# Making the owners of the sorted columns behind the index, instead of ahead of it, in a fused RWKV-5 and switch-routing kernel

## The chip, the cores and the metric

The kernel runs on one core of a Trainium2 chip. The metric is the device time of one execution in microseconds (us), the lower the better. The kernel before was timed three times: 420.32 us in the median, 418.83 the lowest and 420.70 the highest. Its profiled execution took 419.83 us, of which 418.1 us lie between the first and the last instruction; all times "at" some point below count from that first instruction.

The engines are called PE (TensorE, matrix products; PEld is its weight load), DVE (VectorE), ACT (ScalarE), POOL (GpSimd) and SP (SyncE, which issues most of the DMA transfers).

## The reference, cut to what matters

Two blocks stand behind one another. The first is a linear recurrence over 768 steps for 4 batches, 8 heads and a head size of 48. Its output, seen as 3072 tokens of 384 numbers, goes through a gate that sends each token to one of 8 experts, and each expert is a two-layer network of its own weights.

```python
def _attn_ref(r, k, v, w, u):
    ...
    for t in range(S):
        cur = np.einsum('bhd,bhe->bhde', u[None] * kt, vt)
        y[:, :, t] = np.einsum('bhd,bhde->bhe', rt, state + cur)
        state = w[None, :, :, None] * state + np.einsum('bhd,bhe->bhde', kt, vt)
    return y

def _moe_ref(x, w_gate, w1, w2):        # x: 3072 x 384, w1: 8 x 384 x 1024, w2: 8 x 1024 x 384
    logits = x @ w_gate
    expert_idx = np.argmax(logits, axis=1)
    ...                                 # probs: a softmax of the logits
    gate_w = probs[np.arange(N), expert_idx]
    for e in range(E):
        mask = expert_idx == e
        xe = x[mask]
        h = np.maximum(xe @ w1[e], 0.0)
        ye = h @ w2[e]
        out[mask] = gate_w[mask, None] * ye
    return out
```

## The kernel before

The kernel runs the recurrence first, in 32 units, and writes its rows to a table in HBM, `x_hbm`. Then it sorts the tokens by expert and works on them in tiles of 128 tokens. The first two tiles, `t0` and `t1`, are chosen early, from the first half of the batches, and belong to experts 0 and 1, so their rows and weights are loaded while the recurrence still runs. All later tiles, from `t2` on, need the full sort. Two things come out of it on DVE:

- the **index** `idx`: for each column (a tile is one column) the token numbers of its 128 rows. It is built by 24 small matrix products and four DVE operations. The gathers of a tile's rows (POOL's indirect DMA) need it.
- the **owners** `ei`: for each column the expert that it belongs to. They are built by eight DVE operations on one partition. The load of a tile's first-layer weights `w1` (1536 KB) needs them, since SP reads the expert's number from `ei` to make the address; the second product reads the expert's number too, on PE, to pick its slice of `w2_all`.

```python
    def owners(self, rt, first):
        ef = rt.tile([1, NCOL], FP32, name="ef")
        tge = rt.tile([1, NTILE, E], FP32, name="tgo")
        nc.vector.tensor_tensor(tge, ..., op=ALU.is_ge)
        nc.vector.tensor_reduce(ef[:, 0:NTILE], tge, axis=AX, op=ALU.add)
        oe = rt.tile([1, E, E], FP32, name="oe")
        nc.vector.tensor_tensor(oe, self.own[0:1], ..., op=ALU.mult)
        nc.vector.tensor_reduce(ef[:, NTILE:], oe, axis=AX, op=ALU.add)
        self.ei = rt.tile([1, NCOL], I32, name="ei")
        nc.vector.tensor_scalar_min(self.ei, ef, float(E - 1))
        ...                                  # nf, twice, and nt: how many late tiles there are

    def to_index(self, pool, Bv, n, n_chunks, tag, nm):     # R.index calls this
        ...
        for g in range(n_chunks):
            nc.tensor.matmul(idp..., lhsT=self.At[:, g, :], rhs=Bv[:, g]..., ...)
        nc.vector.tensor_copy(idl, idp)                     # idxl
        nc.vector.tensor_scalar(out=emp, ...)               # idxe
        nc.vector.scalar_tensor_tensor(out=raw, ...)        # idxr
        nc.vector.scalar_tensor_tensor(out=idx, ...)        # idx

    def load_w1(self, wp, part=0):
        ...
            e = self.expert(ENG.SP)                         # reads ei on SP
            nc.sync.dma_start(self.w1, w1[ds(e, 1)]...)

    def turn(self, mo, tag, copy=nc.vector.tensor_copy):    # needs the rows xs
        for d in range(DT):
            nc.tensor.transpose(p[:, d, :], self.xs[:, 128 * d:128 * d + 128], ident)
        copy(self.xT, p)

    def hidden(self, mo, fb, within=None, at=2):            # needs xT and w1; fb is 0 or 1
        for f in range(4):
            if within and f == at:
                within()
            for d in range(DT):
                nc.tensor.matmul(p[:, f, :], lhsT=self.w1[:, q, d, o:o + 128], rhs=self.xT[:, d, :], ...)
        nc.scalar.activation(self.hT[:, 4 * fb:4 * fb + 4, :], p, func=ACT.Relu)

    def product(self, within=None):                         # needs hT and w2_all
        for f in range(FT):
            if within and f == FT - 2:
                within()
            nc.tensor.matmul(p, lhsT=self.hT[:, f, :], rhs=w2_all[:, e, f * DM:(f + 1) * DM], ...)

    def weigh(self, mo):                                    # yo, on DVE
        nc.vector.tensor_scalar_mul(self.y, self.p, self.xs[:, DM:W])
```

The seam between the recurrence and the tiles stands in the program in this order. The order of the statements is the order of the instructions on each engine.

```python
            t0.hidden(mo, 1)
            t1.turn(la, "g", nc.scalar.copy)
            R.bases(rt)
            R.order(rt)
            R.slots(rt)
            for step in R.onehots(B - 1):
                step()
            R.owners(rt, NSURE - NEARLY)
            t2.load_w1(wp)
            w2_load(E - 1)
            t0.product()
            t1.hidden(mo, 0, lambda: R.index(rt, "rw"), 3)
            t2.load_x(mo)
            t3.load_x(mo)
            t0.weigh(mo)
            t0.store()
            t1.hidden(mo, 1)
            R.segment_index()
            t3.load_w1(wp)
            t1.product(lambda: t2.turn(mo, "g"))
            t1.weigh(mo)
            t1.store()
            ...
            run_tiles(tiles[2:], ...)      # t2.hidden(0), t2.hidden(1), t3.turn, t2.product, ...
```

Of the kernel before, what the change touches and what calls it, by code (L numbers as in the profile page):

```python
# [20 lines left out]
E, F = 8, 1024  # L21
# [16 lines left out]
NSURE = NG  # L38
FQ = 4
FW = F // FQ  # L40
NEARLY = 2
# [12 lines left out]
def rwkv5_then_switch(ctx, tc, r, k, v, rk, tok, wu_in, wg, wgh, w1, w2, out):  # L54
# [38 lines left out]
    def load_rk(u):  # L93
        b, hf, hp = unit(u)
        if u < 4:
            nc.sync.dma_start(rks[u % 4], rk[b, hf, hp])
        else:
            for hi in range(2):
                q = slice(64 * hi, 64 * hi + D)
                nc.sync.dma_start(rks[u % 4][q], rk[b, hf, hp, q])  # L100

    def load_v(u):
        b, hf, hp = unit(u)
        nc.sync.dma_start(vs[u % 6][:, 0:2 * HC * D], tok[b, hf, hp, :, 0:2 * HC * D])

    def load_kt(u):
        b, hf, hp = unit(u)
        nc.sync.dma_start(kts[u % 4], tok[b, hf, hp, :, 2 * HC * D:])
# [118 lines left out]
    def w2_load(e, eng=nc.sync, q=slice(0, FQ)):  # L227
        eng.dma_start(w2_all[:, e, :].rearrange("p (q f) -> p q f", q=FQ)[:, q], w2[e, q].rearrange("q p f -> p q f"))
# [200 lines left out]
    def fast():  # L429
# [6 lines left out]
        wp = att.enter_context(tc.tile_pool(name="wp", bufs=1))  # L436
# [4 lines left out]
        R = Routes(ps, la, NEARLY)  # L441
# [25 lines left out]
        def scaled(out, tab, hp, by):  # L467
            nc.scalar.activation(out[:, hp, :], tab[:, hp, :], func=ACT.Copy, scale=by[:, hp:hp + 1])

        def tables(hp):  # L470
            scaled(W2, Wr, hp, w_64)
            scaled(W1, Wp, hp, w_64)

        def table_g():
            w3p = ps.tile([128, HP, C], FP32, name="w3p", tag="rw", bufs=1)
            for hp in range(HP):
                nc.tensor.transpose(w3p[:, hp, :], W3[:, hp, :], ident)
            nc.vector.tensor_copy(Wg, w3p.rearrange("p a (h d) -> p a h d", h=2)[:, :, :, 0:D])  # L478
# [23 lines left out]
        def u_scale_first(u):  # L502

            x = units[u]
            hp = x["hp"]
            if u:
                nc.vector.tensor_tensor(x["RK"], x["r"], x["k"], op=ALU.mult)
            for o, i, tab in (("K", "k", Wr), ("R", "r", Wp)):
                nc.vector.scalar_tensor_tensor(out=x[o], in0=x[i], scalar=w_64[:, hp:hp + 1],
                                               in1=bc(tab[:, hp, None, :], [128, HC, C]), op0=ALU.mult, op1=ALU.mult)  # L510
# [10 lines left out]
        def u_scale_g(u):  # L521
            x = units[u]
            hp, ns = x["hp"], x["ns"]
            nc.gpsimd.tensor_tensor(  # L524
                x["Kg"][:, 0:ns, :], x["kt"][:, 0:ns, :],
                bc(Wg[:, hp].rearrange("p h d -> p (h d)")[:, None, :], [128, ns, 2 * D]), op=ALU.mult)
# [32 lines left out]
        def u_scores(u, parts=(u_own, u_products, u_diagonal)):  # L559
            units[u]["P"] = [ps.tile([128, 512], FP32, name=f"P{hi}", tag=f"P{hi}", bufs=2) for hi in range(2)]  # L560
            for part in parts:
                part(u)

        def u_mask(u):
            x = units[u]
            A, P = x["A"], x["P"]
            for hi in range(2):
                nc.vector.copy_predicated(  # L568
                    A[:, hi], bc(mask[:, None, :].bitcast(I32), [128, HC, C]),
                    P[hi][:, 0:HC * C].rearrange("p (c t) -> p c t", t=C))  # L570
# [44 lines left out]
        def gate_weights():  # L615
            nc.gpsimd.memset(IW, 0.0)
            for hi in range(2):
                nc.sync.dma_start(IW[64 * hi:64 * hi + D, :, 2 * D:], wgh[hi])
# [56 lines left out]
        with tc.manual_schedule():  # L675
            u_scale_first(0)
            gate_weights()
            load_rk(4)
            load_v(4)
            for load in pieces[:AHEAD]:  # L680
                load()
            for hp in range(HP):
                scaled(W3, Wr, hp, pw[:, LV - 1])
            u_scores(0, (u_own, u_diagonal, u_products))
            tables(2)
            u_scale_first(1)
            R.begin()
            nc.vector.memset(Gp, 0.0)
            table_g()
            u_mask(0)  # L690
            u_scores(1, (u_own, u_diagonal, u_products))
            u_scale_g(0)
            load_kt(4)
            u_scale_g(1)
            for hp in (3, 0, 1):
                tables(hp)
            u_state(0)
            u_scale_r(2)
            idle(2)
            for u in range(NU):  # L700
                if u + 5 < NU:
                    load_rk(u + 5)
                    load_kt(u + 5)
                    load_v(u + 5)
                for load in piece.get(u, ()):
                    load()
                if u + 2 < NU:
                    u_scale_k(u + 2)
                    if u:
                        u_scale_r(u + 2)  # L710
                    u_scale_g(u + 2)
                if u == 0:
                    u_out(0)
                    u_mask(1)
                    u_state(1)
                elif u + 1 < NU:
                    u_scores(u + 1)
                    u_state(u + 1)
                    u_mask(u + 1)
                if u:  # L720
                    u_out(u)
                if u == 2:
                    gate_columns()
                if u >= HP and u % HP < HC:
                    u_gate(u // HP - 1, u % HP, "rw")
                for step in todo[u]:
                    step()
                for j in range(NEARLY):
                    if u == 2 * HP + j:
                        tiles[j].clear(la)  # L730
                    if u == NU - HP + 2 * j:
                        tiles[j].load_x(la)
            fr.close()
            t0, t1, t2, t3 = tiles[0:4]
            t0.turn(la, "g")
            for c, tag in enumerate(("rw", "y", "y")):
                u_gate(NU // HP - 1, c, tag)
            fy.close()
            rt = att.enter_context(tc.tile_pool(name="rt", bufs=1))
            mo = em.enter_context(tc.tile_pool(name="mo", bufs=2))  # L740
            shift, first, weight, rows = chosen[B - 1]
            product, *ranks = R.ranks(B - 1, "rw")
            shift()
            first()
            t0.hidden(mo, 0, product, 3)
            weight()
            rows(0, 2)
            rows(1, 2)
            for e in range(NW, E - 1):
                w2_load(e)  # L750
            for step in ranks:
# [5 lines that stand above are left out]
            R.slots(rt)  # L757
            for step in R.onehots(B - 1):
                step()
            R.owners(rt, NSURE - NEARLY)  # L760
            t2.load_w1(wp)
            w2_load(E - 1)
            t0.product()
            t1.hidden(mo, 0, lambda: R.index(rt, "rw"), 3)
            t2.load_x(mo)
            t3.load_x(mo)
            t0.weigh(mo)
            t0.store()
            t1.hidden(mo, 1)
            R.segment_index()  # L770
# [4 lines that stand above are left out]
            late = late_tiles_of(R, NSURE - NEARLY)  # L775
            run_tiles(tiles[2:], wp, mo, Segments(R, 0), zip(late, [xbs[1][:, i] for i in range(G)] + [t0.xs, t1.xs],
                                                             strict=True))
# [311 lines left out]
    class Segments(Tile):  # L1089
# [9 lines left out]
        def load(self, mo, i):  # L1099

            q = i % FQ
            if i == 0:
                self.es = [self.expert(ENG.SP, NTILE + self.j * NS + k) for k in range(NS)]
                self.w = {}
            self.w[i] = self.tile(mo, [128, NS, DT * FW], "wq", 2)
            for k, e in enumerate(self.es):
                src = w1[ds(e, 1), q].rearrange("a p d f -> p (a d f)") if i < FQ else \
                    w2[ds(e, 1), q].rearrange("a p f -> p (a f)")
                nc.sync.dma_start(self.w[i][:, k], src)
# [139 lines left out]
    with tc.If(usual > 0) as which:  # L1249
        fast()  # L1250
# [60 lines left out]
```

## Time and profile before

| | |
|---|---|
| median of three runs | 420.32 us |
| span of the profiled execution | 418.1 us |
| PE busy | 403.0 us, 96% of the span |
| PE on the chain of work that ended last | 89% of the span |
| DVE, ACT, POOL busy | 154.0, 127.4 and 151.2 us |
| bytes moved by DMA | 99.00 MB, mean 237 GB/s |
| granted clock of PE | 0.99 |

A profile line of the timeline reads: start, duration, engine, source line, operation, tile written <- tiles read, shapes, count, and in brackets the idle time of the engine before it and what ended that. Of the source lines, L961 to L974 are the owners, L859 the matrix products of the index and L862 to L870 its DVE operations, L1019 the load of `w1`, L228 a load of `w2`, L1040 the gather of a tile's rows, L1046 `turn`, L1061 `hidden`, L1072 `product` and L1076 `weigh`. The weights' tiles appear as `w1s` and `w_all`, the gathered rows as `xs`. The recurrence ends at about 127 us, and the seam lies between there and about 155 us.

### The profile page before, as it was taken

To read this page: it belongs to the slowest core of one execution; us is meant where nothing else is said; L and a number is where in the kernel's file an instruction comes from. 1 tells how busy PE (TensorE), PEld (TensorE's weight loads), DVE (VectorE), ACT (ScalarE), POOL (GpSimd) and SP (SyncE) were. 2 spreads that over 40 slices of the span, in tenths; PEclk is the share of its full clock that TensorE was granted. 3 is DMA by queue.
4 is the path that set the end of the run, shared out by engine and by line. 5 is a ranking of instruction groups with operands and counts; after the bars stand their busy time and mean duration, and the time that the engine had idled before them with its cause. 6 is when DMAs were issued, how large, how long until landed. Compare 5 with 4: busy or idle time off the path is not lost.

```text
span 418.1 us, 10368 instructions
## 1 busy us (share of the span) xinstructions
PE 403.0 (96%) x4057; PEld 333.6 (80%) x4057; DVE 154.0 (37%) x410; ACT 127.4 (30%) x395; POOL 151.2 (36%) x194
## 2 busy tenths in 40 slices
PE   7999999999999989999999999999999999999990
PEld 7899999999999767777788887777878786777770
DVE  6887899999977811111111111110111101111100
ACT  3787777776873211111111101011111100100110
POOL 6897679679750031121111222121222111110100
PEclk9999999999999999999999999999999999999996
DMA  7899999999992998568866686968767675455000
GB/s 247 251 253 261 276 273 302 289 279 297 303 259 102 337 385 311 189 231 328 317 191 221 209 310 201 337 197 294 231 240 249 237 263 188 171 185 173 31 24 27
DMA packets 42944, 99.00 MB, mean 237 GB/s; under 512 B 5189, under 2 KB 16474, under 8 KB 42882
## 3 DMA queue, kind: packets, MB, share of 16 engines
q1 hardware_dynamic: 39024, 86.94, 63.9%
q0 software_dynamic: 3712, 11.23, 9.3%
q8 instruction: 37, 0.61, 0.6%
q14 instruction: 25, 0.20, 0.2%
q10 hardware_dynamic: 146, 0.01, 0.0%
HBM read 88.72 MB, written 9.65 MB: 235 GB/s over the span
## 4 chain that ended last, share of the span: by engine, by line
PE 89%; DVE 4%; DMA 2%; POOL 1%; ACT 1%; issue 1%; POOLq 0%; DVEq 0%
PE hp L1061 29%; PE yp L1072 27%; PE P L536 6%; PE P L546 6%; PE yp L607 5%; PE yp L603 4%; PE rp L638 4%; PE Gp L582 3%; PE xTp L1046 2%; DMA xs<-x_hbm,idx 2%; PE hg L1124 1%; PE yg L1144 1%; DMA wu<-in_w_u_dram 0%; ACT A L557 0%; POOL w_all L443 0%
## 5 line engine op out<-in xcount | busy, mean ns | idle before, releaser
L1061 PEld LDWEIGHTS hp<-xT,w1s 128*128 128x128 f32 x1152 | 133.1, 192 | 10.4 <-issue 4.1
L1061 PE MATMUL hp<-xT,w1s 128*128 128x128 f32 x1152 | 135.2, 276 | 0.0
L1072 PE MATMUL yp<-w_all,hT 128*128 (+1 forms) x384 | 128.0, 486 | 0.0
L1072 PEld LDWEIGHTS yp<-w_all,hT 128*128 128x128 f32 x384 | 71.0, 190 | 44.2
L1063 ACT ACTIVATE hT<-hp 128x512 f32<-128x512 f32 x48 | 28.7, 597 | 230.8 <-PE hp L1061 230.8
L1083 POOL DMA_INDIRECT out_dram<-yo,idx x22 | 22.3, 1011 | 192.0 <-DVE yo L1076 182.5
L557 ACT ACTIVATE A<-ident,dv 128x128 f32<-128x128 f32 x192 | 59.6, 389 | 0.2 <-ACT dv L554 0.2
L1076 DVE TENSOR_SCALAR yo<-yp,xs 128x384 f32<-128x384 f32 x22 | 13.6, 618 | 106.5 <-PE yp L1072 106.5
L1048 DVE COPY xT<-xTp 128x384 f32<-128x384 f32 x23 | 12.8, 555 | 99.7 <-PE xTp L1046 99.7
L607 PE MATMUL yp<-A,w_all 128*64 128x128 f32 x384 | 38.4, 274 | 0.0
L518 POOL TENSOR_TENSOR w_all<-w_all 128x384 f32<-128x384 f32 x30 | 30.7, 1023 | 20.2 <-DMA w_all<-in_r_k_units_dram 4.8
L568 DVE COPY_PREDICATED A<-mask,P 128x384 f32<-128x384 int32 x64 | 35.7, 585 | 4.4 <-ACT A L557 4.0
L1040 POOL DMA_INDIRECT xs<-x_hbm,idx x22 | 21.3, 966 | 31.2 <-DVE yo L1076 24.8
L603 PE MATMUL yp<-w_all,St 128*64 128x128 f32 x320 | 31.9, 274 | 0.0
L519 POOL TENSOR_TENSOR w_all<-w_all,W 128x384 f32<-128x384 f32 x30 | 30.7, 1023 | 0.0
L546 PE MATMUL P<-w_all 48*128 48x128 f32 x384 | 29.5, 286 | 0.5 <-ACT dv L554 0.5
L524 POOL TENSOR_TENSOR Kg<-w_all,Wg 128x288 f32<-128x288 f32 (+1 forms) x32 | 27.3, 855 | 2.4 <-DVE Wg L478 2.4
L536 PEld LDWEIGHTS P<-wu,w_all 48*128 48x128 f32 x384 | 23.9, 187 | 4.3 <-issue 1.6
L536 PE MATMUL P<-wu,w_all 48*128 48x1 f32 x384 | 26.6, 250 | 0.2 <-POOL St L453 0.2
L514 DVE TENSOR_TENSOR w_all<-w_all,W 128x384 f32<-128x384 f32 x30 | 26.1, 869 | 0.0
L607 PEld LDWEIGHTS yp<-A,w_all 128*64 128x64 f32 x384 | 24.6, 137 | 0.3 <-DVE A L568 0.2
L546 PEld LDWEIGHTS P<-w_all 48*128 48x128 f32 x384 | 24.2, 188 | 0.6 <-ACT dv L554 0.6
(170 smaller groups left out, 292.8 us busy)
## 6 DMA issues: line engine op xcount, KB each, us to landing
w1s<-in_moe_w_dram SPq DMA_DIRECT2D x22, 1536.0 KB, 8.4
wq<-in_moe_w_dram SPq DMA_DIRECT2D x32, 384.0 KB, 5.3
w_all<-in_v_k_units_dram SPq DMA_DIRECT2D x64, 144.0 KB, 5.0
w_all<-in_r_k_units_dram SPq DMA_DIRECT2D x56, 144.0 KB, 5.6
w_all<-in_moe_w_dram SPq DMA_DIRECT2D x20, 384.0 KB, 5.8
w_all<-in_moe_w_dram SPq DMA_DIRECT2D x3, 1536.0 KB, 9.5
x_hbm<-xb SPq DMA_DIRECT2D x9, 385.0 KB, 5.6
w1s<-in_moe_w_dram SPq DMA_DIRECT2D x8, 384.0 KB, 5.8
```

Source lines behind the costliest of these rows:

```text
L518: nc.gpsimd.tensor_tensor(x["RK"], x["r"], x["k"], op=ALU.mult)
L519: nc.gpsimd.tensor_tensor(x["K"], x["k"], bc(W2[:, x["hp"], None, :], [128, HC, C]), op=ALU.mult)
L524: nc.gpsimd.tensor_tensor(x["Kg"][:, 0:ns, :], x["kt"][:, 0:ns, :], bc(Wg[:, hp].rearrange("p h d -> p (h d)")[:, None, :], [128, ns, 2 * ...
L536: nc.tensor.matmul(P[hi][:, o:o + 1], lhsT=x["RK"][q, c, :], rhs=wu[q, 1, hp:hp + 1], start=True, stop=True, skip_group_check=True)
L546: nc.tensor.matmul(P[hi][:, c * C:(c + 1) * C], lhsT=x["K"][q, c, :], rhs=x["R"][q, c, :], start=True, stop=True, skip_group_check=True)
L557: nc.scalar.activation(A[:, hi, c, :], ident, func=ACT.Copy, scale=dv[:, hi, c:c + 1])
L568: nc.vector.copy_predicated(A[:, hi], bc(mask[:, None, :].bitcast(I32), [128, HC, C]), P[hi][:, 0:HC * C].rearrange("p (c t) -> p c t", t=C))
L603: nc.tensor.matmul(yp[q, c, :], lhsT=old[:, hi, :], rhs=x["R"][:, c, :], start=True, stop=False, skip_group_check=True)
L607: nc.tensor.matmul(yp[q, c, :], lhsT=vh(x, c, hi, 64), rhs=x["A"][:, hi, c, :], start=old is None, stop=True, skip_group_check=True)
L1061: nc.tensor.matmul(p[:, f, :], lhsT=self.w1[:, q, d, o:o + 128], rhs=self.xT[:, d, :], start=d == 0, stop=d == DT - 1)
L1063: nc.scalar.activation(self.hT[:, 4 * fb:4 * fb + 4, :], p, func=ACT.Relu)
L1072: nc.tensor.matmul(p, lhsT=self.hT[:, f, :], rhs=rhs, start=f == 0, stop=f == FT - 1)
```

## The change

Three statements move down past five others: the owners and the two loads behind them come after the index, the two gathers and the weighing of `t0`. Nothing is added or taken away. Its purpose, in the words of its author, is that the sorted tiles' rows are asked for ahead of their weights.

```diff
@@ -757,14 +757,14 @@
             R.slots(rt)
             for step in R.onehots(B - 1):
                 step()
-            R.owners(rt, NSURE - NEARLY)
-            t2.load_w1(wp)
-            w2_load(E - 1)
             t0.product()
             t1.hidden(mo, 0, lambda: R.index(rt, "rw"), 3)
             t2.load_x(mo)
             t3.load_x(mo)
             t0.weigh(mo)
+            R.owners(rt, NSURE - NEARLY)
+            t2.load_w1(wp)
+            w2_load(E - 1)
             t0.store()
             t1.hidden(mo, 1)
             R.segment_index()
```

On the engines this changes one thing only: on DVE, the eight operations of the owners (L961, L963, L965, L966, L968, L971 twice, L974) now stand behind the four of the index (L862, L864, L867, L870) and behind `t0.weigh` (L1076). The instructions of PE, ACT, POOL and SP keep their order.

## Prediction

> **What bounds the kernel now.** I read the page first, its list of busy times, and then the chain of waits around the seam, the list of waits in the same stretch, and the timelines of DVE, SP and PE there.
>
> ```profile
> PE 403.0 (96%) x4057; PEld 333.6 (80%) x4057; DVE 154.0 (37%) x410; ACT 127.4 (30%) x395; POOL 151.2 (36%) x194
> ```
>
> PE is busy for 403.0 of 418.1 us. A change that leaves its work alone can gain only where PE stands still. The chain of waits from 145.12 us on (start, duration, what) shows such a place:
>
> ```profile
> 145.12 0.63 DVE yo L1076
> 145.75 0.29 issue
> 146.03 6.66 DMA xs<-x_hbm,idx
> 152.69 0.14 issue
> 152.83 0.52 PE xTp L1046 x3
> 153.35 1.29 PE yp L1072 x4
> 154.64 5.36 PE hp L1061 x48
> ```
>
> The chain runs through the gather of t2's rows: issued at 146.03, landed 6.66 us later, and only then can PE turn t2's rows. From there on the chain is PE alone. The list of waits for 126 to 185 us says what this costs PE (who, for what: total, times, longest):
>
> ```profile
> PE xTp L1046 <- DMA xs<-x_hbm,idx: 1.3, 1, 1.3
> ```
>
> So 1.3 us is all that the seam's gather costs; the timeline of PE has it as 1.28 us. Who delayed the gather? DVE's timeline (start, duration) shows the order of the sort's last steps:
>
> ```profile
> 142.73 0.38 DVE L961 TENSOR_TENSOR tgo<-iota_f,pad 1x232 f32<-1x232 f32 x1
> 143.14 0.38 DVE L963 TENSOR_REDUCE ef<-tgo 1x29 f32<-1x232 f32 x1
> ...
> 143.94 0.17 DVE L968 TENSOR_SCALAR ei<-ef 1x37 int32<-1x37 f32 x1
> ...
> 144.26 0.15 DVE L974 TENSOR_TENSOR nt<-nf 1x1 int32<-1x1 f32 x1
> 144.34 0.22 DVE L862 COPY idxl<-idp 128x74 f32<-128x74 f32 x1
> ...
> 144.91 0.20 DVE L870 SCALAR_TENSOR_TENSOR idx<-idxr,idxe 128x37 int32<-128x37 f32 x1
> 145.12 0.62 DVE L1076 TENSOR_SCALAR yo<-yp,xsA 128x384 f32<-128x384 f32 x1
> ```
>
> The owners fill 142.73 to 144.41 and the index follows at once. And PE's own part of the index, in the same timeline:
>
> ```profile
> 143.24 1.00 PE L859 MATMUL idp<-Bv,At 128*128 128x74 bf16 x24
> ```
>
> It ends at 144.24, 0.10 us before the DVE copy of it starts. The owners were thus made in a time in which DVE had nothing else to do. What they release is on SP's timeline:
>
> ```profile
> 144.78 0.39 SPq L1019 DMA_DIRECT2D w1s<-in_moe_w_dram  x1
> 145.23 0.50 SPq L228 DMA_DIRECT2D w_all<-in_moe_w_dram  x1
> 147.71 0.38 SPq L1019 DMA_DIRECT2D w1s<-in_moe_w_dram  x1
> ```
>
> The first is t2's w1, the second the last expert's w2, the third t3's w1. The view of the transfers that start in this stretch gives 8.7 us from issue to landing for the first, so it is there at 144.78 + 8.66 = 153.44; the third takes 14.7, to 162.4. The table of stretches (busy times by engine, granted clock, share and rate of the DMA engines) shows the wires full but for one microsecond:
>
> ```profile
> 144.00:146.00 2.00, 2.00 (x25) 2.00 (x22) 1.62 (x9) 0.60 (x1) 0.00 (x0) 1.00 1.03 397
> 146.00:147.00 1.00, 1.00 (x11) 1.00 (x11) 0.00 (x0) 0.00 (x0) 0.96 (x1) 1.00 0.85 175
> 147.00:150.00 3.00, 3.00 (x15) 2.04 (x14) 0.00 (x0) 1.99 (x9) 1.97 (x3) 1.00 1.01 392
> 150.00:153.50 3.50, 2.22 (x9) 1.15 (x8) 0.11 (x1) 0.00 (x0) 0.00 (x0) 1.00 1.03 402
> ```
>
> At 146 to 147 us the w2 loads issued before the seam run out, and t2's w1, issued at 144.78, comes into flow. PE has its first product of t2 (LDWEIGHTS of L1061) at 154.16, 0.7 us after w1 has landed. There is the second margin of the seam, and it is thin.
>
> [...]the gathers issued at 146.03 and 147.31 beside the weights took 6.7 and 6.5 us, those issued at 167.73 and 178.58, with the wires free, 3.1 and 3.2.
> [...]w1 loads that nothing else ran before took 6.4 to 7.7 us here.
> [...]In the trace the wait for the owners ends and the three loads follow, at 144.78, 145.23 and 147.71.
>
> **The change part by part.**
> *Removed ahead of the index.* The eight owners' operations, 142.73 to 144.41, leave their place. But the copy of idp can't start before PE's last product at 144.24. It starts at 144.34 now, so it gains at most 0.10 us; I take 0.05. The gathers are issued at 145.98 instead of 146.03.
> *The first gather.* Its wires are free now, since the w1 load comes later. It takes 3.2 us as the free ones do and lands at about 149.2, ahead of the time when PE asks for it (PE's earlier product ends at 151.55). The wait of 1.28 us is gone; by this alone PE would reach t2's first product at 154.48 - 1.28 = 153.2.
> *The owners' new place.* They start when yo is nearly through. Before, yo ended at 145.12 + 0.62 = 145.74; less 0.05 and a small overlap I put the start of tgo at 145.65. From the start of tgo to the end of ei it took 144.11 - 142.73 = 1.38 us. So ei is there at 147.03, 2.92 us later than before.
> *The w1 load.* From the end of ei to SP's issue it took 144.78 - 144.11 = 0.67 us (SP reads the number and makes the address). The load is issued at 147.70.
> *Its landing.* The earlier w2 loads are through by then, so it starts in an empty queue. Loads of w1 that did so: issued at 192.57 6.4 us, at 344.55 6.5, at 380.33 6.8, at 250.83 7.7 (with a gather's packets running as it was issued) and at 160.03 8.0 (likewise, with the end of another weight load). Here the second gather and t0's store run beside it. I choose 7.5. It lands at 155.2.
> *The first product of t2.* In the wait for the gather before, PE started 0.14 us after the landing. So 155.2 + 0.14 = 155.34 against 154.48 before: 0.86 us later. The 1.28 us wait for the rows has become a wait for the weights of 155.34 - 153.2 = 2.1 us.
> *Behind it.* The load of w2 for the last expert and w1 of t3 are issued about 0.45 and 1.5 us after t2's w1, at 148.15 and 149.2; before they were at 145.23 and 147.71. At the 400 GB/s of the table, a load of 1.57 MB takes 3.9 us of the wires, so I estimate the two to be through at about 159 and 163.5. t2.product asks for w2 at about 160.2 + 0.9 = 161.1 and t3.hidden for its w1 at about 165.3 + 0.9 = 166.2. Both are in time, and from there PE sets the pace alone, as the chain before shows. Nothing gives the delay back, and nothing adds to it.
> The sum: -1.28 + 2.14 = +0.86, thus about 0.2% of the span. 420.32 + 0.86 = 421.2 us.
>
> **The rivals.**
> *The rows' wait simply goes.* Were w1 to land by 153.2, the kernel would gain the full 1.28 us: 419.0. That needs a landing 5.5 us after the issue. The shortest landing in the whole list of w1 loads is 5.4 us, and that is a piece of 384 KB during the recurrence; the whole loads of 1536 KB in an empty queue took 6.4 at least. At 6.4 the landing is 154.1, and the change comes out even, at 420.1.
> *The queue shifts as a whole.* If w2 and t3's w1 come too late as well, PE waits again, at t2.product or t3.hidden. By the sum above the margins are about 2 and 2.7 us; [...]then 422.5 or more would stand there. Against it: t3's w1 took 14.7 us before, most of it spent behind the other two, and with the first gather out of the way the wires carry less.
> *The owners are hidden, the gather is what matters.* If DVE had been the reason for the late gather, more would come of it: up to 1.7 us earlier. The end of idp at 144.24 speaks against that.
>
> **Range and chances.** The result hangs on the landing of one load. At 6.4 us the change makes -0.2 us, at 7.5 +0.86, at 8.5 +1.9. The three runs before spread from 418.83 to 420.70, so a median may be off by 0.5 or so. I take 419.8 to 422.6. Two per cent are 8.4 us, four times the largest of these effects: 1% for each side, 98% for the same.
>
> **What would show it.** In the profile after, the gather of t2 lands in 3 to 4 us, and the wait of PE's xTp for it is not there any more. The ei operation ends at about 147.0 and SP issues w1s at about 147.7. A new wait stands at the first hp of t2, for the DMA of w1s, of 1 to 3 us, and that product starts at 154.3 to 156.4. Behind it PE has no wait. I am wrong if that product starts before 154.0 (the load was faster than all its like), if a second wait follows at yp or at t3's hp, or if idx comes much more than 0.1 us earlier.

## The result, and the profile after

The changed kernel took 425.97 us in the median of four runs (425.06 to 427.57) against 420.51 of the kernel before, a ratio of 1.0135 with a 95% interval of 1.0086 to 1.0184. Two later measurements of the same kernel, with 16 and 22 runs, gave 1.0064 (1.0041 to 1.0088) and 1.0062 (1.0037 to 1.0087). The ratios leave out runs more than 1.5% above the fastest of their kernel. So it is slower, by some 0.6% or 2.6 us; the first four runs lay high, and the first profile shows one reason for it.

The profile after has a span of 424.1 us, 6.0 more than before. The list of waits from 126 to 200 us has a new line (who, for what: total, times, longest), and the wait for the rows is gone:

```profile
PE hp L1061 <- DMA w1s<-in_moe_w_dram: 2.7, 1, 2.7
```

The chain of waits of the changed kernel from 148 to 172 us (start, duration, what) goes through the weights now, where it went through the rows' gather before:

```profile
148.00 2.68 PE hp L1061 x24
150.68 8.07 DMA w1s<-in_moe_w_dram
158.75 0.14 issue
158.88 7.08 PE hp L1061 x48
165.96 0.33 PE xTp L1046 x3
166.29 5.16 PE yp L1072 x16
```

Two things are to be seen. The load of t2's weights takes 8.07 us and ends the wait. And the 48 hp products behind it take 7.08 us, where the same 48 took 5.36 before, running straight on. DVE's timeline shows where the load's lateness comes from:

```profile
147.29 0.24 DVE L862 COPY idxl<-idp 128x74 f32<-128x74 f32 x1 [1.47 <-PE idp L859]
...
147.88 0.20 DVE L870 SCALAR_TENSOR_TENSOR idx<-idxr,idxe 128x37 int32<-128x37 f32 x1
148.09 0.62 DVE L1076 TENSOR_SCALAR yo<-yp,xsA 128x384 f32<-128x384 f32 x1
148.63 0.38 DVE L961 TENSOR_TENSOR tgo<-iota_f,pad 1x232 f32<-1x232 f32 x1
...
149.83 0.17 DVE L968 TENSOR_SCALAR ei<-ef 1x37 int32<-1x37 f32 x1
```

DVE now stands idle for 1.47 us until PE's index products are done, about the time that the owners used to fill (1.68 us); then come the index, yo and the owners. SP's timeline has the loads behind them:

```profile
150.68 0.39 SPq L1019 DMA_DIRECT2D w1s<-in_moe_w_dram  x1
151.12 0.50 SPq L228 DMA_DIRECT2D w_all<-in_moe_w_dram  x1
152.21 0.38 SPq L1019 DMA_DIRECT2D w1s<-in_moe_w_dram  x1
```

To compare the seam between traces I count from the start of t0's turn, the first L1046 on PE (127.26 before, 130.26 after):

| us behind t0's turn | before | after |
|---|---|---|
| idx made | 17.85 | 17.82 |
| ei made | 16.85 | 19.74 |
| t2's w1 issued | 17.52 | 20.42 |
| t2's rows landed | 25.44 | 21.80 |
| t2's w1 landed | 26.19 | 28.49 |
| first hp of t2 | 27.22 | 28.63 |
| from there to the turn of t3's rows | 5.36 | 6.91 |
| from there to PE's last product | 247.32 | 247.32 |

So 1.41 us of the 6.0 are the longer wait, 1.55 are the slower hp products, nothing comes behind them, and 3.0 stand ahead of t0's turn, where no instruction was changed.

Why the hp products were slower is seen in the clock that PE was granted. In this profile it is 0.50 from 11.80 to 18.63 us and from 158.57 to 161.98, that is for 6.83 and 3.41 us, and 1.00 on both sides; the 139.95 us between the two are 41 times 3.41. The table of stretches is cut in steps of this length, counted back from the change at 158.57 (busy time and count of PE, PEld, DVE, ACT and POOL; then the granted clock, the DMA share and GB/s):

```profile
151.74:155.16 3.42, 3.42 (x14) 2.11 (x13) 0.24 (x1) 0.99 (x6) 0.81 (x1) 1.00 0.92 262
155.16:158.57 3.41, 1.01 (x4) 0.26 (x2) 0.93 (x2) 0.00 (x0) 1.16 (x2) 1.00 1.02 406
158.57:161.98 3.41, 3.10 (x14) 3.13 (x15) 0.00 (x0) 0.00 (x0) 0.84 (x1) 0.50 1.03 410
```

In the stretch 155.16 to 158.57 PE is busy for 1.01 of 3.41 us, 30%, with a gap of 2.7 us at its end. In the next stretch its clock is 0.50, and in the one behind that 1.00 again. That the gap brings the half clock is my reading of this profile; the runs with idle products below test it. "Window" and "border" stand below for such steps of 3.41 us, counted from a change of the clock; that there are borders also where the clock does not change is an assumption.

The page's row of the clock, in slices of 10.6 us, has this event only as an 8 among the 9s, in the sixteenth slice, which is easily passed over; and it has another one at the start, the 6:

```profile
PEclk9699999999999998999999999999999999999997
```

That one, clock 0.50 from 11.8 to 18.6 us, lies at the start of the recurrence and goes with most of the 3.0 us there; 0.5 us had been lost before it, since the first P products start at 8.78 instead of 8.29. Over all thirteen profiles of this case t0's turn comes between 125.75 and 132.51 us, once at 130.55 with a clock of 1.00 in all eight stretches from 0 to 130 us (the run with all w2 loads early). What lies ahead of the seam differs by more than any effect here, which is why the seam is counted from t0's turn.

### The profile page after: what moved, and what is told of

Its sections match the earlier page's. It is cut to its first block, busy times and chain, and to the rows that moved or that the text cites. A ratio compares the mean times of both kernels' runs of the same rounds, so it can differ in the third digit from the quotient of the medians.

```text
span 424.1 us, 10368 instructions
## 1 busy us (share of the span) xinstructions
PE 407.9 (96%) x4057; PEld 338.2 (80%) x4057; DVE 147.8 (35%) x410; ACT 127.8 (30%) x395; POOL 152.1 (36%) x194
## 4 chain that ended last, share of the span: by engine, by line
PE 93%; DMA 3%; SPq 1%; POOL 0%; issue 0%; DVE 0%; POOLq 0%; ACT 0%
PE hp L1061 31%; PE yp L1072 28%; PE P L546 6%; PE P L536 6%; PE yp L607 5%; PE yp L603 4%; PE rp L638 4%; PE Gp L582 3%; DMA w1s<-in_moe_w_dram 2%; PE xTp L1046 2%; PE hg L1124 1%; PE yg L1144 1%; DMA w_all<-in_r_k_units_dram 1%; PE idp L859 0%; PE warm L484 0%; SPq L96 0%
## 5 line engine op out<-in xcount | busy, mean ns | idle before, releaser
L1061 PEld LDWEIGHTS hp<-xT,w1s 128*128 128x128 f32 x1152 | 134.5, 194 | 13.4 <-issue 7.4
L1061 PE MATMUL hp<-xT,w1s 128*128 128x128 f32 x1152 | 136.8, 278 | 2.7 <-DMA w1s<-in_moe_w_dram 2.7
L1076 DVE TENSOR_SCALAR yo<-yp,xs 128x384 f32<-128x384 f32 x22 | 13.6, 618 | 106.5 <-PE yp L1072 106.5
L518 POOL TENSOR_TENSOR w_all<-w_all 128x384 f32<-128x384 f32 x30 | 32.8, 1092 | 20.7 <-PE yp L607 4.0
L519 POOL TENSOR_TENSOR w_all<-w_all,W 128x384 f32<-128x384 f32 x30 | 33.9, 1128 | 0.0
L524 POOL TENSOR_TENSOR Kg<-w_all,Wg 128x288 f32<-128x288 f32 (+1 forms) x32 | 22.9, 715 | 3.5 <-DVE Wg L478 3.0
L514 DVE TENSOR_TENSOR w_all<-w_all,W 128x384 f32<-128x384 f32 x30 | 22.3, 745 | 0.0
```

The costliest lines, as they stand in the source:

```text
L518: nc.gpsimd.tensor_tensor(x["RK"], x["r"], x["k"], op=ALU.mult)
L519: nc.gpsimd.tensor_tensor(x["K"], x["k"], bc(W2[:, x["hp"], None, :], [128, HC, C]), op=ALU.mult)
L524: nc.gpsimd.tensor_tensor(x["Kg"][:, 0:ns, :], x["kt"][:, 0:ns, :], bc(Wg[:, hp].rearrange("p h d -> p (h d)")[:, None, :], [128, ns, 2 * ...
```

## The experiments

Theory A: t2's first product waits for its weights, which the late owners made late; the wait is longer than the old one for the rows, and long enough that PE's clock is halved behind it. The rivals: B, the change slows the start too; C, the slow hp products have another cause than the clock; E, DVE's order as such is what costs; D, on the old wait: the gather is slow for its own sake, and not for the weights beside it.

### The changed kernel again

No edit.

> The changed kernel once more, unaltered. Theory A (the wait for t2's weights lasts 2.7 us instead of 1.3 for its rows, and because it lasts that long the clock of PE is halved for one or two windows of 3.41 us behind it; the half-clock windows at 12 to 19 us of the first profile are not the change's): the wait at the first hp of t2 is 2.5 to 3 us again, a half-clock window of 3.41 us follows it again or not, [...]and the start may well show none. Rival B (the change slows the start too): the half clock at 12 to 19 us is there again in this profile, and not in that of a kernel in which only the seam's order differs in another way. Time 424 to 427 us.

423.60 us in the median of 16 runs, ratio 1.0064 (1.0041 to 1.0088). The wait for w1 is 2.8 us, the clock is 0.50 from 155.30 to 158.71, the 48 products take 7.22 us, and the start has a clock of 1.00 from 8 to 19 us. As theory A has it.

> The changed kernel, unaltered, as the partner of the filled one on the same chip. The wait of PE for t2's w1 lasts 2.7 to 2.9 us again; a half-clock window follows it if a window of 3.41 us holds no more than about 1 us of PE's work (two profiles of it did), and not where the wait is cut in two by a border. Ratio to the kernel before 1.005 to 1.008.

424.51 us, 22 runs, ratio 1.0062 (1.0037 to 1.0087). The chain of this profile:

```profile
146.16 8.75 DMA w1s<-in_moe_w_dram
154.91 0.14 issue
155.04 7.22 PE hp L1061 x48
162.26 0.33 PE xTp L1046 x3
```

The load took 8.75 us, the wait 3.4, longer than expected, and the 48 products take 7.22 us as in the run before. The start again has a clock of 1.00 from 8 to 19 us. B falls: two of three profiles of the changed kernel start at full clock, while the profile of the run with the owners first, below, which lacks the change, has half clock from 11.5 to 18.3 us (0.55 in the mean of 12 to 19) though its recurrence has the same instructions. The 3.0 us at the start of the first profile aren't the change's. What was in the other three of the first four runs, no trace tells.

### Idle products in the wait

```diff
             t1.store()
+            fill = ps.tile([128, 128], FP32, name="fill", tag="rw", bufs=1)
+            for i in range(10):
+                nc.tensor.matmul(fill, lhsT=ident, rhs=ident, start=True, stop=True, skip_group_check=True)
             late = late_tiles_of(R, NSURE - NEARLY)
```

They stand on PE between t1's product and t2's first.

> The changed kernel with ten products of no use (128x128, some 0.22 us each, 2.2 us in all) put on PE into its wait for t2's weights. They lie in idle time. Theory A: the first hp of t2 starts as late as without them, but no half-clock window follows it, so t2's 48 hp products take 5.4 us instead of 7.1 and the time falls by 1 to 2 us against the changed kernel. Rival C (the slow hp products come from the data being late or from something else than the clock): they take about 7 us still, and the time is that of the changed kernel or longer.

Four runs from 420.36 to 428.75 us, ratio 1.0111 (1.0033 to 1.0189), too wide to tell it from the unfilled kernel. The profile has 5.60 us for the 48 products. Twice more, with more rounds:

> The changed kernel with the ten idle products in its wait once more, with more rounds, since four runs from 420.4 to 428.8 said nothing on its time. Theory A: 1 to 2 us under the changed kernel, so a ratio to the kernel before of 1.002 to 1.005, where the changed kernel had 1.0064; no half-clock window at 155 to 162 us in the profile, and hp of t2 takes 5.4 us.

423.73 us, 22 runs, ratio 1.0045 (1.0019 to 1.0070). And on the same chip as the unfilled one:

> The changed kernel with ten idle products in its wait, for the third time, now beside the changed kernel. If the half clock costs its 1.6 us in most runs of the changed kernel, this one is 0.8 to 1.6 us under it, ratio to the kernel before 1.002 to 1.005. If the two take the same time, the half clock is seldom, and the changed kernel's loss is the wait alone.

422.97 us, 22 runs, ratio 1.0039 (1.0018 to 1.0060), against 424.51 and 1.0062 of the unfilled. PE's timeline (start, duration, ..., idle before):

```profile
152.31 2.40 PE L777 MATMUL fill<-ident 128*128 128x128 f32 x20
155.20 5.60 PE L1064 MATMUL hp<-xT,w1s 128*128 128x128 f32 x48 [0.49 <-DMA w1s<-in_moe_w_dram]
```

The first hp comes 28.64 us behind t0's turn, no earlier than in the changed kernel (28.63 to 29.29), but the 48 products take 5.60 instead of 7.1 to 7.2. In each of the three filled profiles they take 5.60 us; in the three unfilled ones 7.08, 7.22 and 7.22, with a clock of 0.50 measured behind the wait of the first two. C falls. In the time the filling is worth 1.5 us by the two medians of the same chip, and 1.0 by the two ratios. The intervals overlap, so the profile carries this, and the time only agrees with it. What is left of the loss, 0.39% or 1.6 us, is close to the 1.4 us by which the first hp is later.

### The weighing behind the owners

```diff
-            t0.weigh(mo)
             R.owners(rt, NSURE - NEARLY)
             t2.load_w1(wp)
             w2_load(E - 1)
+            t0.weigh(mo)
             t0.store()
```

> The changed kernel with t0's weighing behind the owners and the two loads, so that the owners start right behind the index. Theory A: the w1 load of t2 is issued 0.5 us earlier (2.3 us later than in the kernel before instead of 2.9), its wait on PE is 2.1 to 2.3 us instead of 2.7, and the half clock follows more seldom; the time lies 0.5 to 2 us under the changed kernel's. If the order of the gathers and the weights were what costs, and not the owners' lateness, nothing would change.

422.20 us, 20 runs, ratio 1.0030 (1.0006 to 1.0055). ei is made 19.12 us behind t0's turn instead of 19.74, the load lands after 7.59 us, the wait is 1.8 us, a little less than expected, the first hp comes at 27.75, and no half clock follows: 1.00 from 156.24 to 159.65, and 5.60 us for the 48 products. With the owners 0.6 us earlier, and the gathers still ahead of the weights, about half of the loss is gone, by the two ratios of the same chip (1.0030 and 1.0064). The load was 0.5 us shorter than in the first profile of the change, too, so not all of it is the owners'.

### Other weights ahead of t2's

The kernel before, DVE as it was:

```diff
-            t2.load_w1(wp)
             w2_load(E - 1)
+            t2.load_w1(wp)
```

> The kernel before, with nothing changed on DVE (the owners stay ahead of the index), but the load of w2 for expert 7 issued ahead of t2's w1, so that 1536 KB more stand in front of w1 in the queue. Theory A (the arrival of t2's w1 sets its first product, whatever the reason of its lateness): w1 lands at 155 to 156.5 if t0's turn is at 127.3, that is 28 to 29 us behind t0's turn instead of 26.2, and the first hp of t2 comes 0.7 to 1.7 us later than in the kernel before; where the wait gets longer than 2 us, a half-clock window may follow. Time 421 to 424 us. Rival E (DVE's order is what costs): as the kernel before.

Four runs, 425.32 us, ratio 1.0103 (1.0037 to 1.0169); the direction is clear, the size is not. w1 is issued at the time of the kernel before (17.52) but lands at 29.75, 0.75 us behind the end of the expected range, and PE waits 0.5 us for the rows and 3.3 for the weights; the first hp comes 2.67 us later than before, where 1.7 at most was expected. E falls as the only cause: the owners are as early as before, and late weights alone bring the loss. This profile has the longest total wait, 3.8 us, but no half clock, though waits of 2.7, 2.8 and 3.4 us had slow products behind them and waits of 1.3 and 1.8 us had not. The windows of its seam:

```profile
152.81:156.22 3.41, 1.67 (x7) 0.79 (x6) 1.17 (x2) 0.00 (x0) 0.80 (x1) 1.00 1.03 402
156.22:159.63 3.41, 1.84 (x16) 1.87 (x17) 0.00 (x0) 0.00 (x0) 1.19 (x2) 1.00 1.04 404
159.63:163.05 3.42, 3.42 (x33) 3.42 (x32) 0.00 (x0) 0.60 (x1) 0.00 (x0) 1.00 0.28 111
```

By this count a border at 156.22 cuts the wait in two, and each window holds 1.67 us of work or more. An estimate from these windows and from the 1.01 us above is that the work inside one window decides, so that the place of a gap between the borders would count as well as its length; it is argued from this one profile. The window with the old wait of 1.28 us (150.72 to 154.13) held 2.1 us of work in the profile before, and a clock of 1.00 followed.

### The late w2 loads earlier

First experts 5 and 6 only, then 7 too, on the kernel before:

```diff
             shift, first, weight, rows = chosen[B - 1]
+            for e in range(NW, E - 1):
+                w2_load(e)
             ...
             rows(0, 2)
             rows(1, 2)
-            for e in range(NW, E - 1):
-                w2_load(e)
+            w2_load(E - 1)                 # second run only
             ...
             t2.load_w1(wp)
-            w2_load(E - 1)                 # second run only
```

> The kernel before (owners ahead of the index) with the loads of w2 for experts 5 and 6 issued as soon as the recurrence has ended, ahead of the stores of the last rows, into a stretch in which the wires are idle (128 to 133 us). Theory A says that the 1.3 us wait of the kernel before comes from a gather that shares the wires with late weight loads: these are through 4 us earlier, t2's weights land at 151 instead of 153.4, and the gather lands by 151.5 or nearly so; the wait shrinks to 0 to 0.7 us and the time falls by up to 1.3 us under the kernel before. Rival D (the gather is slow for its own sake): the wait stays 1.3 us.

421.19 us, 12 runs, ratio 1.0013 (0.9985 to 1.0040): no difference. w1 lands 1.1 us earlier (25.07), where 2.4 was expected, but the gather takes 6.33 us still and the wait is 1.0. It shares the wires with w1 and w2 of expert 7, which did not move: from 148 to 153 us they carry 404 to 415 GB/s. Theory A had looked at the wrong loads.

> The kernel before with all three late w2 loads moved forward into the idle wires: experts 5 and 6 as soon as the recurrence has ended, 7 right behind the stores of the last rows; the owners stay ahead of the index. Theory A: at the gather's time only t2's w1 is in the queue; w1 lands at 24 to 25 us behind t0's turn (26.2 before), the gather at 23 to 24.3 (25.4 before), PE's wait falls from 1.3 us to 0 to 0.3 and the first hp of t2 comes at 25.9 to 26.3 instead of 27.2. The time lies 1 us under the kernel before's. Rival D (the gather is slow beside any weight load): the gather takes 6 us still, and 0.3 us are gained at most.

420.11 us, 22 runs, ratio 0.9971 (0.9945 to 0.9996): faster than the kernel before. But its chain is not what was expected:

```profile
149.31 6.26 DMA xs<-x_hbm,idx
155.71 0.52 PE xTp L1046 x3
156.23 1.29 PE yp L1072 x4
157.52 5.36 PE hp L1061 x48
```

The gather takes 6.26 us with t2's w1 issued 1.25 us ahead of it and t3's w1 1.7 us behind it; the wait falls from 1.28 to 0.87, and the first hp comes at 26.80, 0.42 us earlier than before. Loads that are issued 1.7 us behind a gather didn't slow it in the changed kernel (3.0 us), so in this profile one load of weights in front goes with a gather of over 6 us, as D was put for this run. The rest of the gain in the median isn't in this profile.

> The changed kernel (owners behind the index) with the three late w2 loads moved forward as in the run with all w2 early. It takes all other weights out of the way, and leaves only the late owners. Theory A: w1 is issued 20.5 to 20.8 us behind t0's turn as in the changed kernel, has the wires alone but for the second gather, lands after 6.4 to 7 us at 27 to 27.7, and the first hp of t2 comes at 27.1 to 27.8: a wait of 1.3 to 2 us, not seldom without a half-clock window; 1.2 to 1.6 us slower than the owners ahead of the index with the same loads, and 0 to 0.8 slower than the kernel before. If the lateness of the owners did not matter once the wires are free, both would take the same time.

The same loads with the change's order: 424.17 us, 20 runs, ratio 1.0065 (1.0042 to 1.0089), no better than the change itself, and 4.0 us slower by the two ratios than the early owners with the same loads (0.9971), where 1.2 to 1.6 was expected. w1 has no other weights in front of it, and takes 8.43 us still; the wait is 3.4 us, and behind it the clock is 0.50:

```profile
155.62:159.03 3.41, 0.69 (x6) 0.72 (x7) 0.00 (x0) 0.00 (x0) 1.99 (x2) 1.00 1.03 412
159.03:162.44 3.41, 3.41 (x18) 3.41 (x18) 0.00 (x0) 0.00 (x0) 0.00 (x0) 0.50 0.69 271
```

My expectation of 6.4 to 7 us for the load was wrong. So the late owners cost the same with the w2 loads out of the way, and these are not why the load takes 8 us. But the wires were not its own: t3's w1 was issued 0.8 us behind it, and from 152.21 to 159.03 they carried 2.7 MB (3.41 us at 372 GB/s and 3.41 at the 412 of the table), of which t2's w1 is 1.57 at most.

### The owners first of all

The opposite of the change, with all w2 loads early:

```diff
             R.order(rt)
+            R.owners(rt, NSURE - NEARLY)
+            t2.load_w1(wp)
             R.slots(rt)
             ...
-            R.owners(rt, NSURE - NEARLY)
-            t2.load_w1(wp)
             t0.product()
-            t1.hidden(mo, 0, lambda: R.index(rt, "rw"), 3)
+            t1.hidden(mo, 0)
+            t1.hidden(mo, 1, lambda: R.index(rt, "rw"), 0)
             t2.load_x(mo)
             t3.load_x(mo)
             t0.weigh(mo)
             t0.store()
-            t1.hidden(mo, 1)
```

> The opposite of the change, on top of the early w2 loads: the owners stand right behind R.order, ahead of the slots, so t2's w1 is issued some 4 us earlier than in the kernel before, at 13 to 14 us behind t0's turn, into idle wires; the index goes into the second half of t1's hidden products, since it comes 1.7 us later. Theory A: w1 lands at 20 to 21 us behind t0's turn, before the gather is issued at 20 to 20.5, and the gather, with the wires free, takes 3.1 to 3.5 us and lands before PE asks for it at 24.1. No wait is left at the seam, the first hp of t2 comes at 25.8 to 26 (27.2 before), and the time lies 1.3 us under the kernel before's, ratio 0.996 to 0.998. If the gather is slow for another reason than the weights beside it, it lands at 26 or later and the kernel is slower than the kernel before.

420.02 us, 22 runs, ratio 0.9968 (0.9945 to 0.9991); the profile's chain at the seam is PE alone:

```profile
150.17 2.75 PE hp L1061 x24
152.92 3.87 PE yp L1072 x12
156.80 0.33 PE xTp L1046 x3
157.12 1.29 PE yp L1072 x4
158.42 5.36 PE hp L1061 x48
```

w1 is issued 13.33 us behind t0's turn and lands at 22.27, after 8.94 us, later than expected: the wires were not idle, for as it was issued, at 145.84, the queue of the loads moved 269 GB/s (145.8 to 146 us), and w2 of expert 7 had been issued at 138.86. The gather, issued 0.64 us later than in the kernel before and 2.9 us ahead of w1's landing, lands after 3.4 us. Neither is waited for, and the first hp comes at 25.75, 1.47 us earlier than before. D in its first sense falls with this: beside the end of a load the gather took 3.4 us, and with a load issued just ahead of it 6.26 to 6.66. Whether this version is better than the one with early w2 loads alone, the intervals don't tell; both beat the kernel before and the changed one.

## Why the prediction was wrong, by its own steps

- *The index is not made earlier.* Right: idx came at 17.82 instead of 17.85 us, where 0.05 to 0.10 was said.
- *The first gather.* Right: it landed after 3.0 us, and its wait was gone. But why the gather took 6.66 us in the kernel before was not shown. There, with w1 in flow, the first packet in the gathers' queue is seen 4.2 us after the issue at 146.03; in the changed kernel, where the wires carry 25 GB/s as it is issued at 149.01, after 1.7. The slow gather started late; why is open.
- *The owners' new place and the w1 load.* Right: ei 2.89 us later, where 2.92 was said; the load issued 0.85 us after ei's start, as before.
- *Its landing.* A term mis-sized: 7.5 us was chosen, and the three profiles of the changed kernel show 8.07, 7.82 and 8.75. That makes the first hp 1.41 to 2.07 us later instead of 0.86. I had leaned on loads that started with nothing beside them; the two of my list that had company took 7.7 and 8.0. The table of stretches shows the difference in the start. A load alone, issued at 344.55 in the kernel before:

```profile
345.55:346.55 1.00, 1.00 (x4) 0.57 (x3) 0.00 (x0) 0.00 (x0) 0.00 (x0) 1.00 0.59 89
346.55:347.55 1.00, 1.00 (x4) 0.57 (x3) 0.00 (x0) 0.00 (x0) 0.00 (x0) 1.00 1.08 353
```

and t2's, issued at 150.68 in the changed kernel:

```profile
152.00:153.00 1.00, 1.00 (x4) 0.57 (x3) 0.00 (x0) 0.76 (x4) 0.55 (x1) 1.00 0.86 146
153.00:154.00 1.00, 1.00 (x4) 0.57 (x3) 0.00 (x0) 0.00 (x0) 0.00 (x0) 1.00 0.91 295
154.00:155.00 1.00, 1.00 (x6) 0.66 (x5) 0.09 (x1) 0.00 (x0) 0.00 (x0) 1.00 0.93 355
```

  The first has 353 GB/s in its third microsecond, the other is at 295 in its fourth. It runs beside t3's gather and t0's store, with two loads of weights close behind. From its issue to its landing the loads' queue moved 1.96 MB and the gathers' 0.59, where the lone load had 1.57 and 0.00. The run with the w2 loads out of the way rules out these, but not t3's w1, which was close behind there too. Which of the three makes the load longer was not tried.
- *Behind it.* This is the step that failed: "Nothing gives the delay back, and nothing adds to it." The wait itself added 1.55 to 1.7 us, through the slow products behind it (7.08 to 7.22 us for 48, against 5.36), in all three profiles of the change. The two misses may hang together: with the load at 7.5 us the wait would have been 2.1 us, and the one measured wait of that size, 1.8 us with the weighing last, had no half clock behind it. None of the signs that I had named for being wrong came up, for they looked for further waits and not for slower work. The range was built from the landing alone, with 8.5 us worth +1.9; with the half clock in it, it would have reached 424.
- *The queue behind.* Right: neither t2's product nor t3's hidden waited, and from t3's turn on both kernels take 247.32 us to PE's last product.
- *The sum.* +0.86 was said. At the seam the first profile has 1.41 + 1.55 = 2.96, and the two larger measurements 2.6 to 2.7. The 5.5 us of the first four runs are not explained by the change; 3.0 of its profile's 6.0 us fall at the start, with a half clock there that other profiles of the same kernel don't have.

## What to carry to other kernels

Where an engine makes two things for two transfers, look first at what it would otherwise wait for: the owners were free, as DVE had to wait for the index anyway, and moving them behind turned free work into a delay of 2.9 us of the longer transfer. Count the larger transfer's whole way, issue to landing in the company it will have, before giving the smaller one the right of way. And a gap on PE can have a second price: here, where it left 1.01 us of work or less in a window of 3.41 us, the window behind it ran at a clock of 0.50. A gap that can't be closed can be filled with idle products, behind which the 48 products took 5.60 us in three profiles of three; in the one compared, the first product behind the gap came where it had been (28.64 us behind t0's turn, 28.63 without).

## What the runs showed of the hardware that was not expected

The half clock of the changed kernel's first profile lasted 3.41 us at the seam and twice that at the start. At the seam it came after windows in which PE had been busy for 0.58, 0.69 and 1.01 us (the change again, its order with all w2 loads early, and the first profile); windows with 1.67, 1.84, 1.99 and 2.13 us were followed by a clock of 1.00 (w2 ahead of t2's w1, twice; the weighing last; the kernel before). At the end, where the last yp products run out, 0.44 us was followed by 0.50 in the kernel before, and 1.96 us by 1.00 in the changed one. A threshold of busy time between 1.01 and 1.67 us, an estimate from these windows, would fit all of them, but it is not the whole rule, for in the recurrence, with its smaller products, the clock was halved behind windows that were far busier. The profile of the filled kernel's second measurement (423.73 us) shows it at 118 us, behind 2.61 us:

```profile
114.59:118.00 3.41, 2.61 (x40) 2.02 (x42) 2.77 (x7) 2.97 (x14) 3.20 (x4) 1.00 0.69 195
118.00:121.41 3.41, 3.41 (x34) 3.28 (x34) 3.24 (x11) 2.01 (x7) 2.18 (x3) 0.50 0.24 76
```

The half clock at the start of the changed kernel's first profile came behind 2.98 us of 3.41 (8.39 to 11.80), while in the kernel before a window with 2.99 us (7.36 to 10.78) was followed by a clock of 1.00. What the chip counts there, these runs don't show.

A gather of 128 rows took 6.66 us in the kernel before and 6.26 in the run with all w2 loads early, each with a load of 1536 KB issued 1.25 us ahead of it. It took 3.0 us in the changed kernel, with the wires at 25 GB/s as it was issued, and 3.4 with the owners first, where such a load was 2.9 us from its landing.
